# Nystrom attention and two gated layers on one core: the first chunk's output products placed ahead of the second chunk's weights in the order of emission

## The chip, the core and the metric

The kernel runs on one core of a Trainium2 chip. The metric is the device time of one launch, in microseconds (us). Matrix products run on PE (TensorE), elementwise work on DVE (VectorE) and ACT (ScalarE), some additions on POOL (GpSimd), and SP (SyncE) issues the loads.

## What is computed

```python
A  = softmax(q k_lm^T / 8)        # q_lm, k_lm: means over 18 neighbouring rows, 32 landmarks
Bm = softmax(q_lm k_lm^T / 8)
C  = softmax(q_lm k^T / 8)
Z  = Bm^T / (norm1(Bm) * norminf(Bm) + 1e-6)
for _ in range(6): Z = 2 Z - Z Bm Z
x  = (A Z C v) as 2304 tokens x 512
x  = (silu(x wg1) * (x wv1)) wo1          # d_ff = 1536
out = (sigmoid(x wg2) * (x wv2)) wo2
```

There are 4 batches of 8 heads with 576 rows of 64 elements each.

## The kernel before

The program is written in steps, and a scheduler turns them into one instruction stream per engine: what is emitted earlier has precedence, and an engine takes the first instruction in that precedence that the scheduler believes ready. On the chip each engine then runs its stream strictly in that order, so an instruction that waits holds up all behind it.

Attention of one batch b is `front(b, g)` for each half g of the heads (landmark means `lm`, transposes `lt` and `tp` by PE, scores `cs`, `bm` and `as`, exponentials `e` on ACT, their transposes `et`, the product with v `cv`) and then `back(b)`, the Newton iteration: seven small PE products `nw`, each followed by a combination on DVE (lines 283, 288, 294) that the next product needs. Its result U (transposed into `UT`) is multiplied into the first layer's weights, so that x itself is never formed.

The first layer works in chunks c of 256 of the 1536 hidden columns. `weights(0, c)` loads raw weights (a tile in three buffers), converts them by two ACT and two DVE operations a piece (lines 324, 327, 329, 333) and leaves `W1[c]` (four pieces) and the output weights `wo` (two pieces, split in a high and a low part). For a chunk c and a batch b:

- `uw_steps(c, b)` (U): eight products `pu` of U with `W1[c]`, evicted into `uw` by ACT and DVE. The eight stand in a fixed order, and they use both of the two PSUM banks of tag "o".
- `gv1_steps(c, b)` (G): eight groups of six products `pg` and `pv`, then silu on ACT (`sg`), the product on DVE (`h`), and its high and low part (`hh`, `hl`).
- `o1_steps(c, b)` (O): eight groups of six products `po`, 128x288 each, evicted into `acc`: for chunk 0 by an ACT copy (line 479), later by an addition on DVE (line 481). For the chunks 0 and 1 the groups go through the two "o" banks in turn.

For the chunks 0 and 1 these steps and the attention of the four batches are emitted from a string of words (line 589): F10 is `front(1, 0)`, B1 is `back(1)`, U10 is `uw_steps(1, 0)` (chunk 1, batch 0), O00 is `o1_steps(0, 0)`; I1 and J1 run the weight conversions of chunk 1 up to `W1[1]` and up to its `wo`. From chunk 2 on, and in the whole second layer, a loop emits the steps.

Of the kernel before, what the change touches and what calls it, by code (L numbers as in the profile page):

```python
# [14 lines left out]
def nystrom_moe_kernel(tc, q, k, v, wg1, wv1, wo1, wg2, wv2, wo2, out):  # L15
# [560 lines left out]
    def emit(word, nw=1):  # L576
# [10 lines left out]

    wfill.extend(weights(0, c) for c in range(2))
    first = (
        "F00 F01 B0 I0 F10 U00 G00 J0 F11 I1 U10 B1 O00 G10 J1 F20 O10 U01 G01 "  # L590
        "F21 U11 B2+F30 O01 G11 F31 U02 O11 G02 B3 U12 O02 G12 U03 O12 G03 U13 O03 G13"
    )
    for w in first.split():
# [78 lines left out]
```

## Time and profile before

| | us |
|---|---|
| median of 3 runs | 907.71 (906.84 to 910.9) |
| the profiled execution's own time | 907.64 |
| its span, first to last instruction | 905.9 |
| PE busy, share of the span | 872.2, 96% |
| DVE busy | 523.4, 58% |
| ACT busy | 396.3, 44% |
| POOL busy | 55.8, 6% |

Busy time counts the engine's instructions; waits, semaphores and the issue of DMAs are not in it. The granted TensorE clock is shown as a share of full speed: 1.00 is 2.4 GHz, 0.50 is 1.2 GHz. Matmuls are pipelined and their ends are modelled, so neighbouring rows may overlap.

### The profile page before, as it was taken

To read this page: it belongs to the slowest core of one execution; us is meant where nothing else is said; L and a number is where in the kernel's file an instruction comes from. 1 tells how busy PE (TensorE), PEld (TensorE's weight loads), DVE (VectorE), ACT (ScalarE), POOL (GpSimd) and SP (SyncE) were. 2 spreads that over 40 slices of the span, in tenths; PEclk is the share of its full clock that TensorE was granted. 3 is DMA by queue.
4 is the path that set the end of the run, shared out by engine and by line. 5 is a ranking of instruction groups with operands and counts; after the bars stand their busy time and mean duration, and the time that the engine had idled before them with its cause. 6 is when DMAs were issued, how large, how long until landed. Compare 5 with 4: busy or idle time off the path is not lost.

```text
span 905.9 us, 16181 instructions
## 1 busy us (share of the span) xinstructions
PE 872.2 (96%) x6604; PEld 744.0 (82%) x6604; DVE 523.4 (58%) x1079; ACT 396.3 (44%) x845; POOL 55.8 (6%) x90
## 2 busy tenths in 40 slices
PE   5778999999999999999999999999999999999997
PEld 4456777789999999999988888888888888888886
DVE  4977665765977678769861153355347236433342
ACT  5688477755653355537643262143125114111111
POOL 4530323000000000000000000000000000000000
PEclk9898999999999999999999999999999999999999
DMA  8666221011611132203010031012004000000132
GB/s 270 178 201 195 80 78 30 3 52 43 177 52 52 48 94 71 71 4 114 24 47 1 1 101 39 1 52 88 1 1 139 1 1 24 1 1 0 47 94 71
DMA packets 27083, 57.68 MB, mean 64 GB/s; under 512 B 4224, under 2 KB 7296, under 8 KB 27008
## 3 DMA queue, kind: packets, MB, share of 16 engines
q1 hardware_dynamic: 25280, 54.28, 20.1%
q10 hardware_dynamic: 1728, 2.36, 1.1%
q8 instruction: 52, 0.85, 0.4%
q14 instruction: 23, 0.19, 0.1%
HBM read 51.90 MB, written 4.72 MB: 63 GB/s over the span
## 4 chain that ended last, share of the span: by engine, by line
PE 89%; DVE 4%; ACT 4%; issue 1%; DMA 1%; SPq 0%; ACTq 0%; DVEq 0%
PE po L62 33%; PE pv L62 24%; PE pg L62 24%; PE pu L62 3%; PE tp L145 1%; PE nw L62 1%; PE cs L62 1%; ACT L453 1%; DMA raw<-in_moe_w_val_dram 1%; PE as L62 1%; PE cv L62 1%; DVE lm L131 0%; DMA kin<-in_k_dram 0%; ACT e L172 0%; PE et L195 0%
## 5 line engine op out<-in xcount | busy, mean ns | idle before, releaser
L62 PE MATMUL po<-hh,wo 128*128 128x288 f32 x768 | 164.9, 303 | 1.4 <-ACT acc L479 0.9
L62 PE MATMUL po<-wo,h 128*128 128x512 f32 x648 | 152.2, 389 | 0.0
L526 DVE TENSOR_TENSOR hf<-hf,pv 128x512 f32<-128x512 f32 (+1 forms) x60 | 38.1, 634 | 194.2 <-PE pv L62 194.2
L62 PEld LDWEIGHTS po<-wo,h 128*128 128x128 f32 x648 | 121.1, 188 | 25.3 <-ACT h L360 0.3
L62 PEld LDWEIGHTS po<-hh,wo 128*128 128x128 f32 x768 | 124.4, 188 | 17.1 <-issue 12.9
L62 PE MATMUL pg<-AH,w 128*128 128x512 f32 (+1 forms) x480 | 136.1, 368 | 0.0
L62 PE MATMUL pv<-AH,w 128*128 128x512 f32 (+1 forms) x480 | 136.0, 368 | 0.0
L62 PE MATMUL po<-hl,wo 128*128 128x288 f32 x384 | 113.5, 297 | 0.0
L525 ACT ACTIVATE hf<-pg 128x512 f32<-128x512 f32 (+1 forms) x60 | 33.2, 553 | 165.7 <-PE pg L62 152.1
L62 PE MATMUL pg<-AH,uw 128*128 128x288 f32 x576 | 100.0, 299 | 0.5 <-ACT uw L360 0.5
L62 PE MATMUL pv<-AH,uw 128*128 128x288 f32 x576 | 97.6, 300 | 2.6 <-ACT sg L453 2.6
L62 PEld LDWEIGHTS pg<-AH,w 128*128 128x128 f32 x480 | 87.3, 188 | 15.5
L62 PEld LDWEIGHTS pv<-AH,w 128*128 128x128 f32 x480 | 87.0, 189 | 15.0
L360 ACT CAST h<-hf 128x512 fp32r<-128x512 f32 (+1 forms) x60 | 34.6, 576 | 124.2 <-DVE hf L526 124.2
L62 PEld LDWEIGHTS pg<-AH,uw 128*128 128x128 f32 x576 | 83.7, 188 | 5.5 <-issue 3.4
L62 PEld LDWEIGHTS pv<-AH,uw 128*128 128x128 f32 x576 | 83.3, 190 | 5.6 <-ACT sg L453 3.1
L547 DVE TENSOR_TENSOR oacc<-po,oacc 128x512 f32<-128x512 f32 x90 | 61.9, 691 | 41.0 <-PE po L62 39.9
L62 PE MATMUL pg<-x1l,w 128*128 128x512 f32 x192 | 74.7, 389 | 0.0
L62 PE MATMUL pv<-x1l,w 128*128 128x512 f32 x192 | 74.7, 389 | 0.0
L62 PEld LDWEIGHTS po<-hl,wo 128*128 128x128 f32 x384 | 72.2, 188 | 0.7 <-DVE uw L361 0.5
L481 DVE TENSOR_TENSOR acc<-po,acc 128x288 f32<-128x288 f32 x128 | 56.4, 454 | 16.1 <-PE po L62 15.6
L324 ACT ACTIVATE cv<-raw 128x512 f32<-128x512 f32 x72 | 48.5, 674 | 26.5 <-DVE cv L333 11.3
(121 smaller groups left out, 1092.1 us busy)
## 6 DMA issues: line engine op xcount, KB each, us to landing
raw<-in_moe_w_out_dram SPq DMA_DIRECT2D x24, 512.0 KB, 4.0
raw<-in_moe_w_gate_dram SPq DMA_DIRECT2D x48, 128.0 KB, 3.2
raw<-in_moe_w_val_dram SPq DMA_DIRECT2D x48, 128.0 KB, 3.2
raw<-in_moe_w_gate_dram SPq DMA_DIRECT2D x24, 256.0 KB, 3.0
raw<-in_moe_w_val_dram SPq DMA_DIRECT2D x24, 256.0 KB, 3.4
kin<-in_k_dram SPq DMA_DIRECT2D x8, 576.0 KB, 4.4
qin<-in_q_dram SPq DMA_DIRECT2D x8, 576.0 KB, 5.5
vin<-in_v_dram SPq DMA_DIRECT2D x8, 576.0 KB, 5.5
```

What stands on the lines that cost most here:

```text
L62: nc.tensor.matmul(o, l, r, start=start, stop=stop, skip_group_check=True)
L145: nc.tensor.transpose(ps[:, j], flat(src[:, 2 * u:2 * u + 2]), ident)
L324: nc.scalar.activation(t0, hiw.bitcast(F32), AF.Copy, scale=2.0 ** -112)
L360: nc.scalar.copy(hi, x)
L453: nc.scalar.activation(sg, pss[0], AF.Silu)
L481: nc.vector.tensor_tensor(sl, ps, sl, op=ALU.add)
L525: nc.scalar.activation(h, pss[0], AF.Sigmoid)
L526: nc.vector.tensor_tensor(h, h, pss[1], op=ALU.mult)
L547: nc.vector.tensor_tensor(acc, ps, acc, op=ALU.add)
```

## The change

The string of words is changed in one line. F11 (the second half of batch 1's front) now precedes J0, and O00 (the first chunk's output products of batch 0) precedes B1, I1 and U10.

```diff
     first = (
-        "F00 F01 B0 I0 F10 U00 G00 J0 F11 I1 U10 B1 O00 G10 J1 F20 O10 U01 G01 "
+        "F00 F01 B0 I0 F10 U00 G00 F11 J0 O00 B1 I1 U10 G10 J1 F20 O10 U01 G01 "
         "F21 U11 B2+F30 O01 G11 F31 U02 O11 G02 B3 U12 O02 G12 U03 O12 G03 U13 O03 G13"
     )
```

The same instructions are issued (one two-column warm-up product of `pu1_0` moves with it); their order moves on PE, DVE, ACT and SP within about the first 130 us, and is the same from there on but for neighbours.

In the rows below a name ends in a buffer number; `po1_0_0` is the first layer's output product for chunk 0 and batch 0, `pu1_0_1` the second half of U W1 for chunk 1 and batch 0, `cs_1_1` and `bm_1_1` belong to batch 1's second half. PE around the scores of batch 1's second half, before:

```order
L145 MATMUL tp_1_1_994<-ident_73,qin1_1_328 128x128 x3
L62 MATMUL cs_1_1_1005<-kq1_1_952,bdq1_1_980 32x288 x4
L62 MATMUL cs_1_1_1011<-kq1_1_952,bdq1_1_980 32x288 x4
L62 MATMUL pu1_0_1_1156<-w1_1_933,ut0_82 32x512
L62 MATMUL pu1_0_0_1155<-w1_1_933,ut0_82 32x512
...
L62 MATMUL bm_1_1_1021<-bdk1_1_949,bdq1_1_980 32x32 x4
L195 MATMUL et_1_1_1033<-ident_73,e1_1_1004 96x128 x3
```

and now:

```order
L62 MATMUL cs_1_1_1005<-kq1_1_952,bdq1_1_980 32x288 x4
L62 MATMUL po1_0_0_1137<-hh1_0_0_876,wo0_0_564 128x288
L62 MATMUL cs_1_1_1011<-kq1_1_952,bdq1_1_980 32x288 x4
...
L62 MATMUL po1_0_0_1155<-hh1_0_0_845,wo0_0_564 128x288 x2
...
L62 MATMUL po1_0_0_1165<-hl1_0_0_900,wo0_0_564 128x288
...
L62 MATMUL po1_0_0_1174<-hl1_0_0_923,wo0_0_564 128x288
L62 MATMUL bm_1_1_1021<-bdk1_1_949,bdq1_1_980 32x32 x4
L195 MATMUL et_1_1_1033<-ident_73,e1_1_1004 96x128 x3
```

The eight `pu1_0` products, which read `w1_1` (the second chunk's weights), stood between the scores and `bm`; in their place stand output products of batch 0. Six of the 48 output products now come before the last three gate and value groups of G00, 30 between the transposes of F11's key rows and `bm`, and 12 between `et` and the Newton iteration; `pu1_0` follows them.

ACT in the same place now (the rows from the third output group on; `acc` are the evictions, `cv0` and `cv1` the conversions of raw weights, `e` the exponentials, `eT` the copies of their transposes):

```order
L479 COPY acc0_2_1144<-po1_0_0_1137 128x288
L324 ACTIVATE cv0_1208<-raw_1146 128x512
L479 COPY acc0_3_1162<-po1_0_0_1155 128x288
L172 ACT_TABLE_LOAD
L172 ACTIVATE e1_1_1004,csm1_1_1002<-cs_1_1_1005,nmx1_1_1003 128x3x3x32
...
L196 COPY eT1_1_1032<-et_1_1_1038 96x384
L327 ACTIVATE cv1_1209<-raw_1146 128x512
...
L324 ACTIVATE cv0_1391<-raw_1206 128x512
L479 COPY acc0_2_1144<-po1_0_0_1188 128x288
L327 ACTIVATE cv1_1392<-raw_1206 128x512
```

The evictions of O00 now stand among the exponentials and conversions of F11 and J1; before, all eight stood after them. Between the last `eT` copy and the eviction of the group before the last stand four conversions.

DVE within batch 1's Newton iteration now (`rw` are the combinations that the next `nw` product needs, `uw` the low parts of U W1, `wo0_1` the second chunk's output weights):

```order
L288 SCALAR_TENSOR_TENSOR rw1_1251<-rw1_1240,nw_1_0_1242 128x192
L230 TENSOR_TENSOR sx1_1_1071<-sx1_1_1071,asm1_1_1295 128x576
L361 TENSOR_TENSOR uw1_0_1_1358<-pu1_0_1_1341,uw1_0_1_1358 128x512
L288 SCALAR_TENSOR_TENSOR rw1_1266<-rw1_1251,nw_1_0_1257 128x192
L233 STREAM_TRANSPOSE sx1_1t_1325<-sx1_1_1071 128x576
L333 SCALAR_TENSOR_TENSOR cv1_1337<-cv0_1336,cv1_1337 128x512
L288 SCALAR_TENSOR_TENSOR rw1_1278<-rw1_1266,nw_1_0_1269 128x192
...
L236 TENSOR_TENSOR AH_86<-sx1_1t_1325,AH_86 128x576
L361 TENSOR_TENSOR wo0_1_934<-cv1_1337,wo0_1_934 128x512
L288 SCALAR_TENSOR_TENSOR rw1_1308<-rw1_1293,nw_1_0_1299 128x192
```

Before, the `uw` parts and both pieces of `wo0_1` were done ahead of this iteration; now the two `uw` parts and five operations of the output weights' conversion stand within it.

## Rows read from the trace of the kernel before

**Rows 1.** The page's engine totals: busy us (share of the span) xinstructions

```profile
PE 872.2 (96%) x6604; PEld 744.0 (82%) x6604; DVE 523.4 (58%) x1079; ACT 396.3 (44%) x845; POOL 55.8 (6%) x90
```

**Rows 2.** Busy time by stretch: PE, PEld, DVE, ACT, POOL, granted clock, DMA, GB/s

```profile
300.00:906.00 606.00, 601.07 (x3341) 519.37 (x3339) 310.38 (x583) 203.49 (x413) 0.00 (x0) 1.00 0.14 41
```

**Rows 3.** Timeline of PE: start us, us, work [idle before, what ended it]

```profile
57.83 1.06 PE L62 MATMUL pv<-AH,uw 128*128 128x288 f32 x6 [2.08 <-ACT sg L453]
...
65.20 1.53 PE L62 MATMUL cs<-kq,bdq 128*32 128x288 f32 x16
70.25 1.96 PE L62 MATMUL pu<-w,ut 64*32 64x512 f32 x16 [3.52 <-DVE w L333]
...
85.40 0.53 PE L62 MATMUL po<-hh,wo 128*128 128x288 f32 x2 [0.95 <-ACT acc L479]
...
86.30 0.69 PE L62 MATMUL pg<-AH,uw 128*128 128x288 f32 x4
```

**Rows 4.** PE by single microseconds: length, PE busy, granted clock, DMA, GB/s

```profile
59.00:60.00 1.00, 1.00 (x8) 0.65 0.72 225
...
62.00:63.00 1.00, 0.95 (x4) 0.65 0.00 0
...
69.00:70.00 1.00, 0.00 (x0) 0.77 1.00 396
...
76.00:77.00 1.00, 1.00 (x54) 0.82 0.00 0
```

**Rows 5.** PE's waits over the whole span: us in total, times, longest us

```profile
PE nw L62 <- DVE rw L283: 1.9, 1, 1.9
...
PE et L195 <- ACT e L172: 1.8, 2, 1.5
```

**Rows 6.** PE by stretches of 2 us, in batch 0's Newton iteration

```profile
32.00:34.00 2.00, 1.29 (x19) 0.50 0.64 193
```

**Rows 7.** The chain that ended last, pieces without overlap: start us, us, what

```profile
61.34 1.29 PE tp L145 x6
...
100.59 0.33 PE tp L145 x3
...
101.05 1.15 PE cs L62 x16
...
107.46 0.84 PE cv L62 x48
108.30 1.06 PE as L62 x72
...
116.32 1.10 PE pu L62 x16
...
457.01 6.40 PE po L62 x48
```

**Rows 8.** Timeline of ACT: start us, us, work

```profile
67.54 0.66 ACT L324 ACTIVATE cv<-raw 128x512 f32<-128x512 f32 x1 [1.55 <-DVE cmx L167]
...
70.06 0.66 ACT L172 ACTIVATE e<-cs,nmx 128x288 f32<-128x288 f32 x1
...
78.65 0.40 ACT L479 COPY acc<-po 128x288 f32<-128x288 f32 x1 [1.17 <-PE po L62]
```

**Rows 9.** Timeline of DVE ahead of and within batch 1's Newton iteration

```profile
81.69 0.75 DVE L236 TENSOR_TENSOR AH<-sx_0t,AH 128x576 fp32r<-128x576 f32 x1
...
89.18 0.35 DVE L288 SCALAR_TENSOR_TENSOR rw<-rw,nw 128x192 f32<-128x192 f32 x1
89.73 1.56 DVE L236 TENSOR_TENSOR AH<-sx_1t,AH 128x576 fp32r<-128x576 f32 x1 [0.20 <-ACT AH L235]
...
92.12 0.34 DVE L288 SCALAR_TENSOR_TENSOR rw<-rw,nw 128x192 f32<-128x192 f32 x1
...
95.63 0.35 DVE L288 SCALAR_TENSOR_TENSOR rw<-rw,nw 128x192 f32<-128x192 f32 x1 [0.40 <-PE nw L62]
```

**Rows 10.** Timeline of POOL in the same stretch

```profile
89.25 1.41 POOL L124 TENSOR_TENSOR ls<-kin 128x576 f32<-128x576 f32 x1
```

## The prediction, made before the run

> **What bounds the kernel.** PE bounds it. The engine totals give it 96% of the span [rows 1], and by stretches it is busy for 601 of the last 606 us at full clock [rows 2]. So there is nothing to win behind 300 us, nor anything to lose while PE keeps its work; what PE saves in the attention stage comes off the end nearly one to one. In PE's timeline the stretch that the change touches shows three long waits [rows 3]: 2.1 us before 57.83 for an activation of G00, 3.5 us before 70.25 for the second chunk's weights, and 0.95 us before 85.40 for an eviction. The view by single microseconds shows what two of them cost besides: the granted clock is at its lower level, 1.2 GHz, from 59.35 to 62.65 and from 69.8 to 76.2 [rows 4] (the two end slices read at 0.65, and those at 0.77 and 0.82, give these points). PE never idles within the second of these stretches, so about 6.4 us of it do 3.2 us of work.
>
> **The sum.** I compare one set of work, from the start of the first wait (57.83 - 2.08 = 55.75) to the point where the eight output groups O00, U10, F11 and the first Newton product are done, 86.30 [rows 3]: 30.55 us before.
>
> Its work at full clock, with prices from the chain, whose pieces do not overlap [rows 7]: 48 output products 6.4; 18 gate and value products at the same 6.40/48 = 0.133 each, 2.4; 22 transposes at 0.33/3, 2.4; `cs` 1.15, `cv` 0.84, `as` 1.06, `pu` 1.1; `bm` and one Newton product, some 0.7 by estimate from the `as` row's many small products; and four gate products before the 86.30, in whose place four transposes of F20 now stand, 0.5. Together 16.6. So before, 14 of the 30.55 us were lost: 6.6 in the three waits, 4.85 to the clock (half of 3.3 and of 6.4), the rest in gaps under 0.4 us.
>
> After the change I expect these losses in the same set.
> - The wait of 2.1 us stays, but six output products move into it: 2.1 - 0.8 = 1.3. The lower clock that followed it may go (gain 1.65) or stay (gain 0). No single gap of the split wait is over 1 us, but after it PE is paced by ACT's copies anyway, so I take the middle and charge 0.8.
> - The wait for the weights goes. Behind the six key transposes, which end at 61.34 + 1.29 = 62.63 [rows 7], PE has 30 output products (4.0), nine transposes and a landmark transpose (1.1) and `cs` (1.15): 6.25 us, to 68.9. It then needs a bank that the first exponential frees. That one ends at 70.06 + 0.66 = 70.7 [rows 8]. ACT now has four evictions of 0.40 more ahead of it, but also one conversion pair less and the 1.55 us idle before 67.54 to put them in [rows 8], so I leave 70.7. PE loses 1.8 there.
> - From 70.7 on the exponentials, their transposes, ACT's copies, `cv`, the DVE scaling and `as` follow one another. That scaling now stands on DVE behind a conversion whose ACT half stands behind both copies. I put the end of it at 74.9 with 2.6 of PE work in the 4.2 us: 1.6 lost.
> - The last two output groups' banks are freed by evictions behind conversions of 0.66 each on ACT [rows 8]; `pu` needs both banks: 0.8.
>
> That is 16.6 + 0.8 + 1.3 + 1.8 + 1.6 + 0.8 = 22.9, so this set is done 7.65 us sooner. The 0.95 us wait and the second stretch at the lower clock are in this.
>
> Some is given back in the next stage. Before, the two `uw` evictions of U10 ran behind `cv`, `as` and the output products. Now nothing but six transposes and one Newton product covers them: two ACT casts and two DVE subtractions of about 0.7 each stand between `pu` and the second term of G10. I charge 1.3. The Newton iteration now shares DVE with the five conversions, and with POOL's sums for F20. A row shows what that can cost: the subtraction of line 236 took 0.75 us at 81.69 and 1.56 at 89.73 [rows 9], where POOL's addition, begun at 89.25, lasted until 90.66 [rows 10]. I charge one such excess, 0.8. The Trainium skill (SBUF — State Buffer, "SBUF: two separate sides") says that a DVE operation with two SBUF inputs and a GpSimd one that reads SBUF exclude each other for a whole instruction. This case's 1.56 us agrees. By that rule both long POOL additions of F20, one after each landmark transpose, would catch an operation, and the end would be 0.8 later, 902.9.
>
> Net: 7.65 - 1.3 - 0.8 = 5.5 us. Against the profiled execution's own 907.64 that gives **902.1**; the median of the runs, 907.71, is 0.07 above that execution. Other edits: F11 ahead of J0 moves nothing on PE up to the first output product, since ACT and DVE convert the `wo` of chunk 0 in the same places as before, ahead of G00's first silu; SP's loads keep their places, except that the second output weights and chunk 2's first pieces wait for raw buffers that ACT empties later. I cost that at nothing, because the conversion that reads them stands after the exponentials; were it uncovered, it would delay the last two evictions, one for one.
>
> By bounds: if the lower clock of the first gap goes entirely and the ACT waits are half what I charge (1.8 + 1.6 + 0.8 halved), the result is 902.1 - 0.8 - 2.1 = 899.2. If the first stretch of low clock stays whole and ACT's evictions push the exponential by their 1.6 us, it is 902.1 + 0.8 + 1.6 = 904.5. Most of my weight lies at 900 to 904.
>
> **Rivals.**
> *The clock falls again.* After the change PE is still idle for some 4 us between 62 and 79, in pieces (1.8 + 1.6 + 0.8). In the trace the waits of 1.9, 2.1 and 3.5 us were followed by a stretch at 1.2 GHz [rows 3 to 6], the longest without one is 1.5 (for an exponential [rows 5]). If two of my pieces join, at the exponential, a stretch like the 6.4 us one comes back. It would cost up to 3.2, less what PE would have waited for ACT anyway; I take 2.2: 904.3.
>
> *DVE becomes the bound of G10 and of the Newton iteration: slower than before.* PE runs its stream in order, so each of the seven `nw` products holds the gate products behind it until DVE delivers. Before, the four steps from 89.18 to 95.63 took 1.61 each; the longest, the one with the 1.56 us row in it, 92.12 - 89.18 = 2.94 [rows 9]. If all six steps took 2.94, that would be 6 x 1.33 = 8.0 more, and with PE half idle the clock may fall as it did in batch 0's iteration, at its lower level at 32 us [rows 6]; a stretch like the 6.4 us one is 3.2 more: 902.1 + 11.2 = 913.3. It decides against the change from 0.9 us a step on without the clock, from 0.4 on with it. For it: five added operations of about 0.7 us. Against it: only every second or third step has two of them, and in the trace DVE idled up to 0.4 us for PE in these steps.
>
> *It is hidden or given back.* Reaching U01 and F21 sooner, PE could find the next loads, scores or conversions late and wait there. Batch 2's keys and queries are released by F11's and F20's transposes, which move little. Then the time stays at 907.6. Against it: the later waits on PE are all short, and from 300 us on there are none of note [rows 2].
>
> **How the numbers follow.** A measurement of this kernel can tell about 0.5%, 4.5 us, from no change. Chances: forecast 0.52, lower clock again 0.20, given back 0.17, slower 0.11. Below 903.2 lie nearly all of the forecast case (0.48) and the better part of the clock case's own spread (0.08): faster 0.56. The slower rival gives 0.11 for slower, the remaining 0.33 is within 0.5%. The range runs from 900.0, a little above the favourable bound, to 907.6, the time of the case that all is given back; it leaves out the slower rival and the best corner, under 2 in 10.
>
> **What would show it.** In the changed profile PE's wait before `pu` of 3.5 us should be gone, with the output products starting near 56 and a granted clock of 1.00 from 63 on. New waits should stand at `bm` or `et` for the exponentials (1 to 2 us), at `as` for DVE's scaling, at the `pu` warm-up for ACT's evictions, and at `pg` for `uw`, none over 2. The output products of chunk 1 should start some 5.5 us sooner than before, and everything behind 300 us should be the old rows, shifted by the gain. Steps of the Newton iteration longer than 2.5 us, or a clock of 0.50 after 69, would prove the rivals; a gain at the end of G10 that has gone by 180 us would prove the third.

## The result and the profile after

The changed kernel took **900.29 us** (median of 4 runs, 900.07 to 900.34), the kernel before beside it 907.53 (906.84 to 910.9): ratio 0.9908, 95% interval 0.989 to 0.9926. A second series gave 899.65 and 0.9902 (0.9886 to 0.9918). The profiled execution took 900.24 us, its span 898.4 against 905.9. So the change makes the kernel faster: by 7.4 us between the two profiled executions, by 7.2 between the medians, by 8.4 by the ratio (6.7 to 10 by its interval). 5.5 were predicted. The median stands just above the low end of the range, 900.0; by the ratio the time is 907.64 x 0.9908 = 899.3, below it.

Executions of one kernel differ by some us along with the granted clock (of the kernel before those with a mean of 0.982 took 909.7 to 911.2 us, the one with 0.994 took 904.7), so the experiments below are compared by their ratio to the kernel before in the same series, with medians beside it.

The page's engine totals of the changed kernel; they answer to [rows 1]:

```profile
PE 869.9 (97%) x6604; PEld 743.2 (83%) x6604; DVE 521.5 (58%) x1079; ACT 396.0 (44%) x845; POOL 56.3 (6%) x90
```

PE has the same 6604 instructions and is busy 2.3 us less. Timeline of PE in the changed kernel, the rows that answer to [rows 3]:

```profile
55.15 0.95 PE L62 MATMUL pg<-AH,uw 128*128 128x288 f32 x6
56.66 0.80 PE L62 MATMUL po<-hh,wo 128*128 128x288 f32 x4 [0.56 <-ACT hh L360]
57.95 0.53 PE L62 MATMUL po<-hl,wo 128*128 128x288 f32 x2 [0.50 <-DVE hl L361]
...
62.81 0.30 PE L135 MATMUL lt<-ident,lm 128*128 128x128 f32 x1 [0.60 <-ACT kq L146]
...
70.61 0.27 PE L62 MATMUL bm<-bdk,bdq 128*32 128x32 f32 x8 [0.91 <-ACT e L172]
71.16 0.53 PE L195 MATMUL et<-ident,e 128*96 128x128 f32 x3 [0.29 <-ACT e L172]
...
74.28 0.65 PE L62 MATMUL as<-bdk,kq 128*32 128x64 f32 x32 [0.33 <-DVE bc L203]
...
77.79 1.09 PE L62 MATMUL pu<-w,ut 64*32 64x512 f32 x16
78.81 0.93 PE L145 MATMUL tp<-ident,kin 128*128 128x128 f32 x6
...
81.22 0.53 PE L62 MATMUL nw<-rw 32*32 32x96 f32 x16 [0.89 <-DVE rw L283]
81.69 0.33 PE L135 MATMUL lt<-ident,lm 128*128 128x128 f32 x1
82.16 0.66 PE L62 MATMUL pg<-AH,uw 128*128 128x288 f32 x3
...
92.73 0.69 PE L62 MATMUL cs<-kq,bdq 128*32 128x288 f32 x8
```

The waits of 2.08, 3.52 and 0.95 us are gone. In their place stand six (up to 74.28), none over 0.91. `pu` starts without any, and takes 1.09 where it took 1.96 [rows 3]. The set of work of the prediction runs from 55.15 + 0.95 = 56.10 to 78.81: 22.7 us against 30.55.

Busy time by stretch (us, PE, PEld, DVE, ACT, POOL, granted clock, DMA share, GB/s). First the set in the kernel before, then in the changed kernel, with the stage behind it:

```profile
55.75:86.30 30.55, 23.16 (x270) 17.23 (x269) 23.12 (x57) 24.66 (x56) 7.30 (x10) 0.83 0.68 198
```

```profile
56.10:78.80 22.70, 19.34 (x271) 14.76 (x270) 16.22 (x43) 21.19 (x53) 7.86 (x13) 1.00 0.64 192
78.80:92.70 13.90, 12.87 (x169) 10.36 (x161) 13.26 (x28) 10.22 (x22) 8.10 (x10) 1.00 0.53 145
```

This is where the time came from. PE's idle time in the set fell from 30.55 - 23.16 = 7.4 us to 22.70 - 19.34 = 3.4, by 4.0; its busy time for the same work fell from 23.16 to 19.34, by 3.8, and the mean clock rose from 0.83 to 1.00. Neither of the two low stretches [rows 4] is left.

The stage behind it, up to the next scores. Before, it ended with these scores at 101.02, ahead of which stood nine output products (1.2 us) that now come later, so 99.82 is the like point: 99.82 - 86.30 = 13.52 us. Now it is 92.73 - 78.81 = 13.92. So 0.4 was given back, not 2.1. Behind it 0.6 more is gained up to 179 us (batch 3's second Newton product starts at 178.94 before and at 171.26 now); part of that is less waiting (before, 0.85 for `uw` at 115.17, now no wait there). From there to the last output products (895.21 before, 887.52 now) the rows are the old ones, 7.7 us sooner, and the end of the span, behind the last product, comes 0.2 later in relation to it. The sum: 7.85 in the set, 0.35 lost because it starts later (56.10 for 55.75), 0.4 given back, 0.6 gained behind, 0.2 lost at the end: 7.5, the difference of the spans.

### The profile page after: what moved, and what is told of

Read it like the earlier page. It is cut to its first block, busy times and chain, and to the rows that moved or that the text cites. A ratio compares the mean times of both kernels' runs of the same rounds, so it can differ in the third digit from the quotient of the medians.

```text
span 898.4 us, 16184 instructions
## 1 busy us (share of the span) xinstructions
PE 869.9 (97%) x6604; PEld 743.2 (83%) x6604; DVE 521.5 (58%) x1079; ACT 396.0 (44%) x845; POOL 56.3 (6%) x90
## 4 chain that ended last, share of the span: by engine, by line
PE 90%; DVE 5%; ACT 2%; issue 1%; DMA 0%; ACTq 0%
PE po L62 34%; PE pg L62 25%; PE pv L62 25%; PE pu L62 3%; PE tp L145 1%; PE nw L62 1%; PE cs L62 1%; DVE cv L329 1%; PE as L62 0%; DVE lm L131 0%; DMA kin<-in_k_dram 0%; PE cv L62 0%; PE et L195 0%; DVE w L333 0%; DVE asm L226 0%
```

## Experiments

Two comparisons of the order of instructions needed no run. With F11 ahead of J0 alone, every engine's order is that of the kernel before; with O00 moved alone and J0 left ahead of F11, it is that of the changed kernel. All that follows is O00's move.

**The clock without the move.** The kernel before, with products in its waits that nobody reads. Rival theories: the low clock cost TensorE its half, or ScalarE and VectorE paced those stretches anyway.

```diff
+SX[b, g, 'm'] = cmx
...
 mm(pss[0][:, 0:2], ident, ident[:, 0:2])
+if (c, b) == (1, 0):
+    mm(pss[0][:, 0:2], ident, SX[1, 1, 'm'])   # cmx of F11
+    for _ in range(7):
+        mm(pss[0][:, 0:P], ident, ident)
```

> The kernel before, with 1 two-column product and 7 products of the identity, whose result nobody reads, put on TensorE ahead of the second chunk's U W1 products, in the 3.52 us wait for the second chunk's weights. No other instruction of this stretch moves; the wait itself ends when it did. It keeps TensorE from pausing for over 1.5 us and undoes nothing else. Theory (the clock): the clock stays at 1.00 from 69 to 76, where before it was at 0.50 for 6.4 us with TensorE never idle; that stretch is then shorter by 2 to 3.2 us, and the kernel takes 904.4 to 905.6 against 907.6. Rival (ScalarE and VectorE pace that stretch, the clock costs nothing there): the clock is held, but TensorE waits for exponentials, copies and scalings instead, and the time is 907.2 to 907.7. If the clock falls all the same, the run tells nothing of its price.

Measured: 906.37 us, ratio 0.9974 (0.9963 to 0.9985), so 2.4 us faster by ratio. Stretches and timeline of PE in this run:

```profile
59.00:63.00 4.00, 3.00 (x21) 2.77 (x22) 3.55 (x7) 2.81 (x8) 2.37 (x4) 1.00 0.40 121
69.00:76.00 7.00, 5.11 (x77) 3.59 (x73) 5.12 (x13) 6.28 (x15) 1.34 (x3) 1.00 0.84 254
```

```profile
57.66 0.95 PE L62 MATMUL pg<-AH,uw 128*128 128x288 f32 x6
59.89 1.06 PE L62 MATMUL pv<-AH,uw 128*128 128x288 f32 x6 [1.27 <-ACT sg L458]
...
64.92 0.30 PE L135 MATMUL lt<-ident,lm 128*128 128x128 f32 x1 [1.36 <-ACT kq L146]
...
70.21 0.38 PE L62 MATMUL pu<-cmx,ident 128*128 128x2 f32 x2 [1.18 <-DVE cmx L168]
70.46 1.81 PE L62 MATMUL pu<-ident 128*128 128x128 f32 x14
72.19 1.09 PE L62 MATMUL pu<-w,ut 64*32 64x512 f32 x16
```

The clock was held, and the rival (no gain) falls, but the gain is at the low side of the theory: a stretch at half clock is not worth its half here. Part of the time saved becomes waits for ScalarE (1.36 ahead of 64.92, 0.71 ahead of 74.65), and the unread products themselves hold `pu` back by 0.4 (the last conversion ends at 71.08 + 0.69 = 71.77, `pu` starts at 72.19).

The profile says the same by the set of work: from 57.66 + 0.95 = 58.61 to 85.90 it takes 27.3 us, 3.3 less than before. It starts 2.9 us later, because in this execution batch 0's attention ran at 0.50 from 45 to 55 us. The first wait was 1.27 in place of 2.08, 0.8 of the 3.3, and no low clock followed it, so the run does not separate the first stretch cleanly from the second. The next one adds six products behind the first wait:

```diff
...
 H1[c, b, ft, th] = (hi, lo)
+if (c, b, ft, th) == (0, 0, 0, 0):
+    ps = ptile([P, HS], "n", "fill")
+    for x in (hi, hi, hi, lo, hi, lo):
+        mm(ps, AH[:, 0, 0:P], x)
```

> As the run before it, and besides six products of the first output product's operands, whose result nobody reads, in the 2.08 us wait of TensorE at 55.75 us, in the place where the change has six output products. Theory (the clock): the stretch at 0.50 from 59.35 to 62.65 goes too, worth up to 1.65 us more than the run before it, so 902.8 to 905 in all. The prediction took 0.8 of the 1.65. Rival (after that wait TensorE is paced by ScalarE's copies): the same time as the run before it, within 0.4 us, and waits of TensorE for copies in place of the slow products.

Measured: 904.36 us, ratio 0.9965 (0.9951 to 0.9979), 3.2 us faster by ratio. The point is 0.8 us under the run before it, but the two intervals overlap: what the first stretch is worth stays open between nothing and 2 us. Together the two runs show that the clock alone, with the waits left in place, gives some 3 us (2.4 and 3.2 by the ratios, the latter 1.9 to 4.4 by its interval) of the 8.4 that the change gives by the ratio; the busy times above say 3.8 of 7.4. The rest is the waits themselves, filled with work that had to be done anyway.

**The weights first.** Must the output products stand ahead of the conversion of the second chunk's weights?

```diff
-F11 J0 O00 B1 I1 U10 G10
+J0 F11 I1 O00 U10 B1 G10
```

> The changed kernel, with chunk 0's output products of batch 0 ahead of the second chunk's U W1 products, but behind the conversion of that chunk's W1 in precedence (J0 F11 I1 O00 U10 B1). ScalarE and VectorE then convert W1 first and empty the output products' banks later, and U W1 can start before all output products are done. Theory (what counts is that output products fill TensorE's waits): most of the gain stays, 900 to 902, a wait for weights of under 1 us. Rival (the conversions must stand behind the output products, or banks are freed too late): the two banks of the output products fill up, TensorE waits for their evictions and the clock falls again: 902.5 to 905.

Measured: 904.41 us, ratio 0.995 (0.9933 to 0.9967). About half of the gain is lost, as the rival's times say, but not by its clock, which is 1.00 in every stretch from 55 us on. Waits of TensorE in that run (us in total, times, longest), 53 to 112 us:

```profile
PE pg L62 <- DVE uw L361: 2.0, 1, 2.0
PE po L62 <- ACT acc L479: 1.1, 3, 0.5
PE bm L62 <- ACT e L172: 0.9, 1, 0.9
PE cv L62 <- ACT eT L196: 0.7, 1, 0.7
```

The banks are freed later, as the rival said (1.1), and besides a wait of 2.0 for the `uw` parts of U W1 appears; U10 precedes the Newton iteration here, as in the next run, which tries that alone. By the ratios that costs 2.0 of the 4.4 us lost here, which leaves some 2.4 for the conversions that stand ahead, both uncertain by 1.5. So it matters what the output products pass.

**U W1 ahead of the Newton iteration.**

```diff
-O00 B1 I1 U10 G10
+O00 I1 U10 B1 G10
```

> The changed kernel with the second chunk's U W1 products of batch 0 ahead of batch 1's Newton iteration in precedence (I1 U10 B1 in place of B1 I1 U10). Theory of the give-back (uncovered castings and subtractions of U W1 cost TensorE 0.9 + 0.3 us after it): the castings start sooner, and up to 1.2 us come off: 899.1 to 900.0. Rival (what is saved there is waited for at the Newton products, as the costs in this stretch are moved and not added): 900.0 to 901.0, the waits for the Newton steps longer by as much.

Measured: 902.13 us, ratio 0.9924 (0.9909 to 0.994): about 2 us more than the changed kernel, worse than both theories had it. Timeline of PE:

```profile
79.95 0.40 PE L62 MATMUL pg<-AH,uw 128*128 128x288 f32 x1 [0.76 <-ACT uw L360]
...
82.03 0.67 PE L62 MATMUL pg<-AH,uw 128*128 128x288 f32 x3 [0.88 <-DVE uw L361]
```

Here `uw` is uncovered: 1.64 us in two waits. This is the cost that the prediction had charged the changed kernel with (1.3); there a Newton product and transposes stand between `pu` and the second term of `pg`, which waits no more than 0.14 (81.69 + 0.33 = 82.02 to 82.16).

**The meeting of GpSimd and VectorE, in both kernels.** In the changed kernel the subtraction of line 236 takes 1.89 us, beside one of GpSimd's long additions. Timelines of VectorE and GpSimd, answering to [rows 9] and [rows 10]:

```profile
78.33 0.68 DVE L329 SCALAR_TENSOR_TENSOR cv<-cv,cv 128x512 uint32<-128x512 uint32 x1
...
79.01 1.89 DVE L236 TENSOR_TENSOR AH<-sx_0t,AH 128x576 fp32r<-128x576 f32 x1
80.83 0.34 DVE L283 TENSOR_TENSOR rw<-nw,rr 128x192 f32<-128x192 f32 x1
...
83.68 0.34 DVE L288 SCALAR_TENSOR_TENSOR rw<-rw,nw 128x192 f32<-128x192 f32 x1
...
84.63 1.03 DVE L333 SCALAR_TENSOR_TENSOR cv<-cv,cv 128x512 uint32<-128x512 uint32 x1
85.58 0.34 DVE L288 SCALAR_TENSOR_TENSOR rw<-rw,nw 128x192 f32<-128x192 f32 x1
...
87.36 0.78 DVE L236 TENSOR_TENSOR AH<-sx_1t,AH 128x576 fp32r<-128x576 f32 x1
```

```profile
78.36 1.93 POOL L124 TENSOR_TENSOR ls<-kin 128x576 f32<-128x576 f32 x1
...
83.69 1.42 POOL L124 TENSOR_TENSOR ls<-qin 128x576 f32<-128x576 f32 x1
```

The Newton step behind it (line 283) is what TensorE waits 0.89 for at 81.22. The same edit was made to both kernels; it leaves out the sums of batch 2's first half:

```diff
-x = sm("ls", [P, NU, D], 1)
+x = src
+if (b, g) != (2, 0):
+    x = sm("ls", [P, NU, D], 1)
...
```

> The changed kernel without four of GpSimd's additions for each of the two landmark sums of batch 2's first half: the landmark is taken from two of the eighteen rows, so those landmarks are wrong, and no other engine's instructions move. It takes away what lies beside the 1.89 us subtraction of line 236. Theory of the prediction (the meeting of the two engines costs TensorE 0.8 in this stage): that subtraction takes 0.75, the first Newton step comes 1.1 sooner, TensorE's 0.9 wait for it goes, and 0.5 to 1.0 us come off the changed kernel: 899.3 to 899.8. Rival (the Newton steps have slack, or the next wait takes its place): 900.0 to 900.5.

> The same additions taken out of the kernel before (the same landmarks wrong). There the subtraction of line 236 took 1.56 at 89.73 us. Theory A (the prediction's: only the changed kernel pays for this meeting, the kernel before hides it): before stays where it is, within 0.3 us. Theory B (the kernel before pays for it as well, so the prediction charged a cost that was moved and not added): 0.5 to 0.8 us come off the kernel before too, and the changed kernel's gain is the same with the additions and without.

Measured: changed kernel 897.61 us, ratio 0.9878 (0.9861 to 0.9895), against 0.9902 with the sums in the same series; kernel before 907.26, ratio 0.9978 (0.9967 to 0.999). So some 2.2 and 2.0 us, each uncertain by 1: **theory B**. The change is worth 0.9878 / 0.9978 = 0.990 without the sums and 0.9902 with them. Timeline of PE, changed kernel without the sums, and the subtraction on VectorE:

```profile
78.41 0.93 PE L147 MATMUL tp<-ident,kin 128*128 128x128 f32 x6
...
79.87 0.53 PE L62 MATMUL nw<-rw 32*32 32x96 f32 x16
...
90.95 0.69 PE L62 MATMUL cs<-kq,bdq 128*32 128x288 f32 x8
```

```profile
78.61 0.74 DVE L238 TENSOR_TENSOR AH<-sx_0t,AH 128x576 fp32r<-128x576 f32 x1
```

The stage takes 90.95 - 78.41 = 12.5 us, 1.4 less. In the kernel before, with the sums, PE waited 0.70 for a Newton step at 92.52; without them, the wait is gone:

```profile
92.52 0.53 PE L62 MATMUL nw<-rw 32*32 32x96 f32 x16 [0.70 <-DVE rw L288]
...
101.02 1.18 PE L62 MATMUL cs<-kq,bdq 128*32 128x288 f32 x16
```

```profile
86.20 0.70 PE L62 MATMUL pg<-AH,uw 128*128 128x288 f32 x4
...
100.16 1.18 PE L62 MATMUL cs<-kq,bdq 128*32 128x288 f32 x16
```

The upper fence is the kernel before, the lower one that without the sums: 100.16 - 1.2 - 86.20 = 12.8 us, 0.8 less than 13.5. So without the meeting the stage is as long after the change as before it (12.5 and 12.8), and nothing of `uw` or the conversions is given back. With it the stage costs 1.4 and 0.8 more: the give-back is that difference, 0.6, less 0.2. One correction to the edit's reading: GpSimd runs ahead of the other engines, so the additions that meet line 236 are those of batch 2's second half, not of its first, as the prediction and the expectation had it. Without the first half's sums they start 12 us sooner. The edit also takes away sums at 55 to 59 us, and in the changed kernel the 0.50 wait at 57.95 goes with them (one of 0.36 for ScalarE follows); its set of work becomes 0.7 us shorter, so more comes off than the 1.0 at most that was expected. In the kernel before, the profiles account for 0.9 of the 2.0 us; where the rest comes from is open.

**Versions that might beat both.** Two and three buffers for the landmark let GpSimd run further ahead, with all outputs computed:

```diff
-lm = sm("lm", [P, 2, D], 1)
+lm = sm("lm", [P, 2, D], 2)
...
```

> The changed kernel with two buffers in place of one for the landmark (and one in place of two for three small tiles that VectorE alone uses, to make room). All outputs are computed. GpSimd need not wait for TensorE's transpose of the landmark before it goes on to the next sum, so the long additions of batch 2's second half no longer start at 78.4 us, beside the 1.89 us subtraction of line 236. Theory (the run without those sums gained 2.0 us because the meetings were gone): TensorE's 0.9 wait before its second Newton product goes, 0.5 to 1.5 us come off the changed kernel's 899.65 to 900.3: 898.2 to 899.7. Rival (the sums, sooner, meet other subtractions of VectorE or the conversions): 899.7 to 901, with an operation of VectorE elsewhere at 1.3 us or more in place of 0.75.

> The changed kernel with three buffers for the landmark (two small tiles of the normalisation share the buffers of the Newton iterate to make room). All outputs are computed. With two buffers the key sum of batch 2's second half moved 14 us ahead, but the query sum took its place beside the subtraction of line 236, which stayed at 1.89 us, and so did TensorE's 0.9 wait. With three, the query sum should go at some 68 to 72 us, and nothing of GpSimd's be left at 76 to 81. Theory (the meeting at line 236 costs the changed kernel 0.9): that subtraction takes 0.75, the wait goes, 0.7 to 1.2 us come off the run with two buffers' 899.0: 897.8 to 898.4. Rival (the next wait takes its place, or the sum meets something else): 898.8 to 900.3.

Measured with two: 899.02 us, ratio 0.99 (0.988 to 0.9919); the next sum took the place beside line 236 (1.89 us again), as the rival has it; the median lies in the theory's range, but by the ratio (0.99 against 0.9902) no gain is shown. With three: 899.01, ratio 0.9894 (0.9873 to 0.9915). There the meeting is gone and so is the wait at the Newton product, and in the profile the stage takes 90.29 - 77.24 = 13.05 us, 0.9 less, but the gain does not stand out of the noise in the time. In its profile another wait has grown and a further subtraction (line 361, 0.68 alone) now meets a sum at 1.92. VectorE, then PE:

```profile
77.44 0.74 DVE L236 TENSOR_TENSOR AH<-sx_0t,AH 128x576 fp32r<-128x576 f32 x1
...
84.94 1.92 DVE L361 TENSOR_TENSOR wo<-cv,wo 128x512 fp32r<-128x512 f32 x1
```

```profile
72.70 0.65 PE L62 MATMUL as<-bdk,kq 128*32 128x64 f32 x32 [1.17 <-DVE bc L203]
```

So the meeting can be moved, but no version here is shown to beat the changed kernel: the ratios of all lie within its interval. What it costs that small tiles share or give up buffers to make room for the landmark was not measured by itself. The same holds for holding the clock in batch 0, alone and with two landmark buffers:

```diff
 ps = prod(RW)
+if b == 0 and it in (3, 4):
+    fl = ptile([P, 96], "o", f"fill{it}")
+    for _ in range(4):
+        mm(fl, flat(RW)[:, 0:P], RW[:, 0])
...
```

> The changed kernel with products whose result nobody reads in batch 0's Newton iteration: four behind each of its steps 4 and 5 and two ahead of the first U W1 products, in TensorE's pauses between 39.5 and 44.4 us. After those pauses the changed kernel's clock is at 0.50 from 43.4 to 50.0, and from 45 to 50 TensorE is never idle. Theory (the clock is worth its half wherever TensorE has its work ready): clock 1.00 there, 1.5 to 2.8 us saved: 897.5 to 898.8. Rival (ScalarE, 0.97 busy there, paces it): 899.8 to 900.6. A third way: the products push the Newton products back, 900.6 to 902.

> The run before it together with the unread products in batch 0's Newton iteration, which alone gave 899.45 where the changed kernel had 900.3. If the two gains have separate causes they add: 0.8 us under the run before it, 897.4 to 898.9. If ScalarE and VectorE pace batch 0's stretch whatever the clock: the same time as the run before it, within 0.4 us.

Measured: 899.45 us, ratio 0.9901 (0.9881 to 0.9921), and 899.89, ratio 0.9896 (0.9879 to 0.9914). The clock was held. First the changed kernel's stretch, then that of the run with the products alone:

```profile
43.00:50.00 7.00, 5.93 (x59) 3.19 (x60) 5.36 (x13) 4.97 (x15) 0.00 (x0) 0.52 0.74 238
```

```profile
43.00:50.00 7.00, 5.76 (x147) 3.77 (x151) 5.88 (x15) 6.09 (x15) 0.00 (x0) 1.00 0.67 225
```

By the medians 0.8 us of that reach the end, by the ratios nothing that is clear of the uncertainty, and ScalarE is busy 6.09 of the 7 us where it was busy 4.97. From 50 to 55 us PE is then busy 4.55, where it had been busy throughout. In the profiles the piece from U00's `pu` to the start of the set takes 54.55 - 43.83 = 10.72 us with the clock held and 56.10 - 44.38 = 11.72 without, so about 1 us came back there, less than the 1.5 to 2.8 of the theory: most of this stretch is paced by the other engines, as the rival has it, but not all.

**The same move one batch later.**

```diff
-F21 U11 B2+F30 O01 G11
+F21 O01 U11 B2+F30 G11
```

> The changed kernel, with the same move one batch later: chunk 0's output products of batch 1 ahead of the second chunk's U W1 of batch 1 and of batch 2's Newton iteration (F21 O01 U11 B2+F30 G11 in place of F21 U11 B2+F30 O01 G11). Between 92 and 181 us the changed kernel's TensorE waits for 2.9 us in all, no wait over 0.9, at a clock of 1.00. Theory (the move pays only where TensorE waits and the clock falls behind it): no gain, 900 to 901. Rival (output products ahead are better in themselves): 898.5 to 899.5. A third way (they are then missing beside batch 2's Newton iteration, where they fill TensorE's pauses): 901 to 905, with new waits before the Newton products.

Measured: 902.2 us, ratio 0.9922 (0.9907 to 0.9938), about 2 us slower than the changed kernel: the third way. PE's busy time from 110 to 135 us, changed kernel and then this run, and a new wait:

```profile
110.00:135.00 25.00, 24.47 (x358) 19.90 (x346) 16.92 (x47) 19.18 (x44) 6.17 (x13) 1.00 0.18 49
```

```profile
110.00:135.00 25.00, 22.06 (x310) 17.97 (x309) 17.09 (x44) 15.25 (x40) 5.43 (x9) 1.00 0.18 49
```

```profile
133.19 0.40 PE L62 MATMUL pg<-AH,uw 128*128 128x288 f32 x1 [0.86 <-ACT uw L360]
```

Where there was no long wait to fill, output products sent ahead only leave later waits open (for `uw`, for the first Newton step). Output products ahead are not better in themselves.

## Why the prediction was right, and where it failed

- *PE bounds, and what it saves in the attention stage comes off the end.* Right: 7.1 us sooner at 92.73, 7.7 at the last products, 7.5 at the end; the rows behind 179 us are the old ones, shifted.
- *The set is done 7.65 us sooner.* Measured 7.85. That the sum held is luck: two of its terms were off by nearly the same in opposite directions. The work was taken as 16.6 us at full clock, at prices from long rows of products; PE was busy 19.34. The prediction booked 2.5 us of the set before to short gaps and charged nothing for them after, though the six waits (3.19) leave 22.70 - 16.6 - 3.19 = 2.9 unexplained by work. The waits were taken as 6.3 with the low clock; PE idled 3.36. By term: the first wait kept 0.56 + 0.50 for the 1.3, the low clock after it went altogether (0.8 charged), PE waited 0.91 for the first exponential (1.8 charged; it ended at 70.5, not 70.7), 0.29 + 0.33 in the chain behind it (1.6 charged), and nothing of note ahead of `pu` (0.8 charged); a wait of 0.60 for a copy of key transposes, at 62.81, had no term. The second low stretch was read a little short: by finer slices it is 69.5 to 76.4, and PE idles in it until 70.25, which leaves its price as good as unchanged (half of 3.4 + 6.1 is 4.75, for 4.85).
- **The step that failed: "Some is given back in the next stage", 2.1 us.** It measured 0.4. The 1.3 for the `uw` castings and subtractions is not there: `pg` waits 0.14 at most for them, and without the meeting the stage is no longer than before. The Newton product and the transposes cover it, as the run that puts U10 ahead of the Newton iteration shows by uncovering it (1.64). The 0.8 for one meeting at line 236 was charged in full, though the row cited for its price, the 1.56 us subtraction [rows 9], is itself such a meeting in the kernel before, which paid 0.8 for it in the same stage. The meeting moved; it was not added. What the change adds is the difference, some 0.6.
- *The Trainium skill's rule* (SBUF — State Buffer, "SBUF: two separate sides": a VectorE operation with two SBUF inputs and a GpSimd one that reads SBUF exclude each other for a whole instruction) is borne out by this trace: 1.89 beside an addition, 0.74 without. GpSimd's own addition grew too, from 1.41 [rows 10] to 1.93; it began at 78.36, within the conversion of line 329 (78.33 to 79.01), which also has two inputs in SBUF, so by the times it was itself held first. Both long additions caught an operation, as the prediction had it by that rule, but the second, at 83.69, caught the conversion of line 333 (1.03 where 0.65 to 0.68 is usual), and no wait of TensorE stands behind it; the 902.9 did not come.
- *The low end.* The text's own favourable bound was 899.2, and the range was cut at 900.0 above it. With the give-back at 0.4 the sum is 902.1 - 1.7 = 900.4, close to the median; by the ratio the time lies at 899.3, under the range.
- *The clock falls again.* No: PE's idle pieces never joined, the longest is 0.91, and the clock is 1.00 from 51 to 300 us. *DVE becomes the bound.* No: the steps of line 288 are 1.5 to 1.9 us apart, not 2.9. *Hidden or given back later.* No: nothing more of the gain is lost up to 179 us.

## What to carry to other kernels

A long wait of TensorE is worth its own length and part of what the clock loses behind it; read both from the busy and idle time of the whole set of work, rather than halving the low stretch. Before charging a change with a cost that a row of the old kernel shows, ask whether the old kernel already pays it in the same stage: then only the difference counts. And work sent ahead pays where there is a wait to fill; elsewhere it is taken from a later one.

## What the runs showed of the hardware

- The granted clock fell behind pieces of idle time that were each short: in the run with both waits filled, PE's longest wait between 64 and 69 us was 1.36, it was busy 3.04 of these 5 us, and the clock read 0.79 there and 0.50 behind. The prediction's reading, that waits of 1.9 us and more were followed by a fall and none up to 1.5, was too simple; it also left out the 7.17 us ahead of PE's first product, with a clock that reads 1.00 before and behind them. The stretch with the wait and the microsecond behind it:

```profile
64.00:69.00 5.00, 3.04 (x18) 1.61 (x22) 3.30 (x6) 4.71 (x12) 3.14 (x4) 0.79 0.69 225
69.00:70.00 1.00, 1.00 (x12) 0.20 (x4) 0.57 (x2) 0.34 (x1) 0.92 (x2) 0.50 0.76 208
```

- The same wait of 1.36 in the run with only the second filled was followed by no fall. Whether the clock falls at a given place also differs between executions of kernels whose order is the same there: from 45 to 50 us it was 1.00 in the profile of the kernel before and 0.50 in that of the changed kernel.
- A stretch at half clock cost between a tenth of its length and two fifths: in batch 0 some 6.8 us of it, which the profile of the kernel before does not have, made the piece from U00's `pu` to the start of the set 0.6 us longer (11.72 for 55.75 - 44.62 = 11.13), and 1.0 longer than with the clock held; in the attention of batch 1 the two stretches of the kernel before, 9.5 us with PE at work, were worth 3.8.
